# Forming sixteen MLP pieces inside the gelu pauses, and moving the normalising products from GpSimd to VectorE

## The chip, the cores and the metric

The kernel runs on one core of a Trainium2 chip. The metric is the device time of one execution in microseconds (us); lower is better. Five engines work side by side, each through its own instructions in order: TensorE (PE in the profile, PEld for its weight loads), VectorE (DVE), ScalarE (ACT), GpSimd (POOL) and SyncE (SP), which here only issues DMA transfers. Matmul results land in PSUM, eight banks of 128 partitions by 512 float32 values; GpSimd doesn't read PSUM here.

## The reference

An attention block and an MLP, both on the same layer-normalised input, and their sum.

```python
xn = _layernorm(x)                                   # x: 1 x 2048 x 512
# A: 32 heads of 16
qkv = (xn @ wqkv).reshape(B, S, 3, 32, 16).transpose(2, 0, 3, 1, 4)
p = softmax(einsum("bhqd,bhkd->bhqk", q, k) * 16 ** -0.5)
A = einsum("bhqk,bhkd->bhqd", p, v).transpose(0, 2, 1, 3).reshape(B, S, D) @ wo
# B: 512 -> 1792 -> 512
h = gelu(einsum("bsd,df->bsf", _layernorm(xn), w1) + b1, approximate=True)
return x + A + einsum("bsf,fd->bsd", h, w2) + b2
```

## The kernel before, in words

The attention is cut into 32 groups `g`: 4 query tiles `qt` of 512 queries, times 8 sets of 4 heads. A group has 16 key blocks of 128, and a unit is one head's 128 x 512 scores for one key block; there are 2048 units. A score pass (`qk`, line 1165; its matmul is line 1169) forms up to four units at once in different row strips of the array. A unit goes one of two ways.

- **ScalarE's way.** `build_tile` (1334) puts two or three units side by side in the scores' banks 0 to 4 and one ACTIVATE (line 1374) takes the exponentials.
- **VectorE's way.** `build_dve` (1459) takes a set of four units: each is shifted to integers from its bank (line 1471), then `dve_terms` makes three shifted copies of all four (line 1492, 2048 int16 columns), and the four versions are read as float16 and added up by four passes over the values. The scores of such a set ride along in a score pass of ScalarE's units, or go alone (`ride_alone`, 1299), and need a bank of the pool `misc` (banks 5 to 7).

Both end in `pv` (1179; matmul line 1187), which accumulates a group's output and its row sums in a `misc` bank. `build_opost` (1516) finishes a group: the bank is copied to `osb` (1527), the row sums go to DRAM and back as `lc`, VectorE takes reciprocals `rc` (1534), these go to DRAM and come back broadcast as `rlb`, and a product `osb * rlb` (1543) gives the normalised heads. That product is on GpSimd for the first 28 groups and on VectorE for the last three that pass here.

The MLP works on the same query tiles. `build_mlp` (1633) forms 14 pieces for each `qt`: `chain` (937) makes a piece's four matmul steps (sixteen matmuls, line 606) in a `misc` bank, and VectorE adds `b1` and writes it to `ht` (line 1655). The weights come through a ring of four buffers (`w1_r`, `NW1`). After every second query tile `fg` (1664) runs gelu in place over the 28 pieces of two tiles, as four ACTIVATEs of 3584 columns; exponentials stop for that time. `merge` (1688) multiplies by `w2` (and `wo`) and adds `acc`, which `sums` (1675) has filled by two GpSimd transfers for each 128 rows: `x`, and `b2` added in flight.

A planner (`_Plan`, `run` at 134) fixes the order of all instructions when the kernel is built: it simulates the engines with planned durations (0.60 us and more on VectorE, `GMUL = 2.1` for the product on GpSimd, `L1, L2, L3` for the transfers), and takes on each engine the ready operation of the least due time; the table `PICK` overrides single choices by their count on the engine. While TensorE would pause, `fill` (1783) issues matmuls over zeros (line 1813), and `zeros` (1322) adds one beside score passes (1329).

Of the kernel before, what the change touches and what calls it, by code (L numbers as in the profile page):

```python
# [11 lines left out]
ALU = mybir.AluOpType  # L12
# [48 lines left out]
class _Plan:  # L61
# [72 lines left out]
    def run(self):  # L134
        free = self.free = {e: 0.0 for e in self.ENGS}
        self.count = {e: 0 for e in self.ENGS}
# [6 lines left out]
        while self.left:  # L143
            best = None
            for e in self.ENGS:
# [7 lines left out]
                every = cand  # L153
# [3 lines left out]
                if e == "PE":  # L157
# [4 lines left out]
                    if hot:  # L162
# [5 lines left out]
                key = lambda c: (c[1].prio + self.nudge(c[1].seq)  # L168
                                 - (self.KEEP if c[1].mode == same else 0.0), c[1].seq)
                t, op = min((c for c in cand if c[0] <= first + tol), key=key)  # L170
                want = self.pick.get(e, {}).get(self.count[e])
                if want is not None:
                    t, op = next((c for c in every if c[1].seq == want), (t, op))
# [5 lines left out]
            self.count[op.eng] += 1  # L179
# [43 lines left out]
    nudge = staticmethod(lambda seq: 0.0)  # L223
# [264 lines left out]
def kernel(  # L488
# [133 lines left out]
    def act(cols):  # L622
# [10 lines left out]

    wide = {key: _Pool([res[i]]) for key, i in (
# [51 lines left out]
    TLAT, YP, YLAT = 2.6, 6.0, 4.2  # L686
    ZROW = 1
    DG = (3,)
    GMUL = 2.1
    YB = 17.0  # L690
# [17 lines left out]
    KT1, QT1 = 45.0, 55.0  # L708
    KTP, QTP = 55.0, 75.0
    HOT = 4  # L710
    XACT = 2
    F2 = 200.0
    CHUNK = 4
    HOLD = 75.0
# [1155 lines left out]
```

## Time and profile before

| | |
|---|---|
| median of 3 runs | 778.33 us (778.17 to 778.48) |
| profiled execution | 776.0 us, of which the span of instructions 774.2 us |
| busy, share of the span | PE 95%, ACT 96%, DVE 92%, POOL 14% |
| exponentials on ScalarE, line 1374 | 623 instructions, 702.2 us |
| VectorE's own sets, lines 1471 and 1492 | 520 and 390 instructions, 620.6 us |
| gelu on ScalarE, line 1669 | 8 instructions, 24.9 us, and two table loads of 1283 ns |
| products on GpSimd, line 1543 | 28 instructions, 39.2 us |

A row of instruction groups says line, engine, operation, written tile, read tiles and shapes, count, then the busy time, the mean duration of one in ns, and the idle time just before them. A matmul's end is modelled and matmuls overlap, so PE's 95% isn't its share of useful work. Neighbouring instructions of an in-order engine overlap a little too, so the distance between two starts is shorter than a duration.

### The profile page before, as it was taken

The numbers are of one execution on the slowest core, as the hardware profiler recorded it, in microseconds if no ns is written. First come the engines' busy times: TensorE is split into PE (matmuls) and PEld (weight loads), VectorE is DVE, ScalarE is ACT, GpSimd is POOL, SyncE is SP. The second block draws the span as 40 slices with busy tenths as digits, with TensorE's granted clock in tenths as the row PEclk, the third lists the DMA queues.
The fourth block names the chain that finished last, engine by engine and source line by source line (L and its number), as shares of the span: only waits on it lengthen the run. The fifth ranks groups of instructions, "written<-read, shape, count | busy, mean of one in ns | idle before, by whom it ended". The sixth has DMA issues, their size and how long they took to land.

```text
span 774.2 us, 23564 instructions
## 1 busy us (share of the span) xinstructions
PE 736.0 (95%) x10064; PEld 247.5 (32%) x10066; DVE 708.5 (92%) x1191; ACT 740.1 (96%) x651; POOL 105.5 (14%) x139
## 2 busy tenths in 40 slices
PE   8999999999999999999989999999999999999996
PEld 3434333333323323333322333323323223333332
DVE  8999999889999998998989998989999997899993
ACT  6999999999999999999998999999999999999995
POOL 5610101000021101000032000000213000110010
PEclk9999999999999999999999999999999999999998
DMA  6327111202323121100183211031332002122001
GB/s 218 71 70 171 56 46 42 64 18 60 90 50 74 55 56 36 39 25 30 39 163 78 49 31 39 18 93 50 88 90 59 18 19 56 53 72 53 17 16 34
DMA packets 77150, 46.56 MB, mean 60 GB/s; under 512 B 53429, under 2 KB 68213, under 8 KB 77041
## 3 DMA queue, kind: packets, MB, share of 16 engines
q1 hardware_dynamic: 70544, 33.48, 16.9%
q0 software_dynamic: 5536, 11.01, 5.6%
q8 instruction: 79, 1.29, 0.7%
q10 hardware_dynamic: 960, 0.52, 0.2%
q14 instruction: 31, 0.25, 0.1%
HBM read 30.01 MB, written 7.19 MB: 48 GB/s over the span
## 4 chain that ended last, share of the span: by engine, by line
PE 45%; DVE 24%; ACT 20%; issue 8%; DMA 2%; SPq 0%; POOL 0%; DVEq 0%; ACTq 0%
ACT p_sb L1374 20%; PE ps L1169 15%; PE ps L1187 15%; PE ps L606 13%; DVE x_sb L1471 10%; DVE it L1492 8%; DVE it L1471 1%; DMA lc<-ldram 1%; DMA ldram<-osb 1%; DVE ht L1655 1%; PE ps L1813 1%; DVE osb L1527 1%; PE ps L1742 0%; PE ps L611 0%; DVE ot L1693 0%
## 5 line engine op out<-in xcount | busy, mean ns | idle before, releaser
L1374 ACT ACTIVATE p_sb<-ps 128x1536 bf16<-128x1536 f32 (+1 forms) x623 | 702.2, 1257 | 18.7 <-PE ps L1169 16.0
L1169 PE MATMUL ps<-qz,kt 32*128 32x512 bf16 x2048 | 307.0, 383 | 20.0 <-ACT p_sb L1374 7.1
L1471 DVE TENSOR_SCALAR x_sb<-ps 128x512 int16<-128x512 f32 x412 | 274.1, 684 | 14.3 <-PE ps L1169 12.7
L1492 DVE TENSOR_SCALAR it<-x_sb 128x2048 int16<-128x2048 int16 x309 | 218.0, 722 | 4.1 <-PE ps L1187 2.3
L1169 PEld LDWEIGHTS <-kt 32*128 32x128 bf16 x2048 | 80.6, 91 | 257.7 <-issue 250.9
L1187 PE MATMUL ps<-p_sb,va 128*32 128x512 bf16 x1528 | 149.7, 389 | 2.0 <-DVE ht L1655 1.2
L1187 PE MATMUL ps<-it,va 128*32 128x512 f16 x1668 | 135.8, 381 | 2.1 <-DVE it L1492 2.0
L1187 PEld LDWEIGHTS <-va 128*32 128x32 bf16 x3608 | 78.0, 95 | 140.7 <-issue 114.8
L1329 PE MATMUL ps<-ones_bf,zeros_bf 32*128 32x512 bf16 x272 | 100.0, 383 | 0.0
L1471 DVE TENSOR_SCALAR it<-ps 128x512 int16<-128x512 f32 x108 | 72.9, 684 | 8.2 <-PE ps L1169 8.0
L606 PE MATMUL ps<-yT,w_r 128*32 128x512 bf16 x896 | 59.2, 384 | 2.8 <-DVE it L1471 1.6
L606 PE MATMUL ps<-w_sb,ht 128*32 128x512 bf16 x896 | 59.7, 381 | 0.0
L1492 DVE TENSOR_SCALAR it<-it 128x2048 int16<-128x2048 int16 x81 | 55.6, 702 | 0.6 <-PE ps L1187 0.3
L1543 POOL TENSOR_TENSOR ons<-osb,rlb 128x512 bf16<-128x512 f32 x14 | 19.4, 1383 | 238.1 <-DMA rlb<-rdram 145.6
L1543 POOL TENSOR_TENSOR ont<-osb,rlb 128x512 bf16<-128x512 f32 x14 | 19.8, 1418 | 217.3 <-DMA rlb<-rdram 196.4
L1655 DVE TENSOR_SCALAR ht<-ps,b_sb 128x512 bf16<-128x512 f32 x56 | 41.7, 745 | 1.1 <-PE ps L606 0.9
L1187 PE MATMUL ps<-x_sb,va 128*32 128x512 f16 x412 | 41.1, 385 | 1.5 <-DVE x_sb L1471 0.9
L1813 PE MATMUL ps<-ones_bf,zeros_bf 128*32 128x512 bf16 x468 | 39.7, 384 | 0.0
L606 PEld LDWEIGHTS <-w_r 128*32 128x32 bf16 x896 | 22.1, 96 | 26.3 <-issue 13.2
L1329 PEld LDWEIGHTS <-zeros_bf 32*128 32x128 bf16 x272 | 24.0, 91 | 19.3 <-issue 18.6
L606 PEld LDWEIGHTS <-ht 128*32 128x32 bf16 x896 | 20.2, 96 | 24.8 <-issue 11.5
L1669 ACT ACTIVATE ht<-ht 128x3584 bf16<-128x3584 bf16 x8 | 24.9, 3178 | 0.0
(101 smaller groups left out, 336.2 us busy)
## 6 DMA issues: line engine op xcount, KB each, us to landing
rlb<-rdram SPq DMA_DIRECT2D x31, 256.0 KB
w_r<-in_B_w_dram SPq DMA_DIRECT2D x56, 128.0 KB
wkv<-in_A_x_dram POOLq DMA_DIRECT2D x16, 256.0 KB, 3.6
wkv<-in_B_b_dram POOLq DMA_DIRECT2D x16, 256.0 KB, 4.2
qz<-zdram SPq DMA_DIRECT2D x30, 128.0 KB
ydram<-ys POOLq DMA_DIRECT2D x16, 128.0 KB, 2.1
zdram<-qc SPq DMA_DIRECT2D x15, 128.0 KB
w_sb<-in_B_w_dram SPq DMA_DIRECT2D x1, 1792.0 KB
```

Of the source, the lines that this page charges most:

```text
L606: I(nc.tensor.matmul(dst[32 * j:32 * j + 32], lhsT=lhsT[:, 32 * j:32 * j + 32], rhs=rhs, start=start, stop=stop, tile_position=(0, 32 * j)))
L1169: I(nc.tensor.matmul(ps[:, bank, :], lhsT=kt[lo:lo + 32, s // 2, k * P:(k + 1) * P], rhs=qz[lo:lo + 32, (qt * NB + s // 2) % NQB, s % 2, : ...
L1187: I(nc.tensor.matmul(ps[32 * j:32 * j + 32, o_bank[g], :], lhsT=vals[:, h * VS:h * VS + 32], rhs=wts(j), start=pv_done[g] == 1, stop=end, ...
L1329: I(nc.tensor.matmul(ps[:, o_bank[g], :], lhsT=zeros_bf[32 * j:32 * j + 32, :], rhs=ones_bf[32 * j:32 * j + 32, :], start=False, stop=Fals ...
L1374: exp_inst.append(I(nc.scalar.activation(p_sb[:, s0:s1, :].rearrange("p a b -> p (a b)"), ps[:, b0:b0 + n, :].rearrange("p a b -> p (a b)" ...
L1471: I(nc.vector.tensor_scalar(out=ib[sl][:, j, :], in0=ps[:, pool.bank(key), :], scalar1=LEVEL, scalar2=0.0, op0=ALU.add, op1=ALU.max))
L1492: I(nc.vector.tensor_scalar(out=tb[x].rearrange("p j q -> p (j q)"), in0=ib[sl].rearrange("p j q -> p (j q)"), scalar1=float(SHIFT[t]), sc ...
L1527: e0 = add("DVE", dve(QW), lambda: I(nc.vector.tensor_copy(osb[:, i2, :], ps[:, o_bank[g], :])), pvs + before, pr - 1000, rel=(o_done(g),))
L1543: lambda: I((nc.vector if late else nc.gpsimd).tensor_tensor(out=dst, in0=osb[:, i2, :], in1=rlb[:], op=ALU.mult)), [e3] + list(free),
L1655: I(nc.vector.tensor_scalar(out=hq[:, fc, :], in0=ps[:, misc.bank(key), :], scalar1=b1_sb[:, fc:fc + 1], scalar2=None, op0=ALU.add))
L1669: I(nc.scalar.activation(out=hv, in_=hv, func=AF.Gelu_apprx_tanh, scale=1.0))
L1813: I(nc.tensor.matmul(ps[32 * j:32 * j + 32, bank, :], lhsT=zeros_bf[:, 0:32], rhs=ones_bf[:], start=new, stop=new, tile_position=(0, 32 * ...
```

## The change

- **Pieces during gelu.** Of the 14 pieces of query tiles 1 and 3, the last eight (`ND`), sixteen in all, aren't formed before gelu any more. They are formed after the gelu instructions have begun, in the scores' banks 0 to 4 (pool `idle`), and ScalarE reads them there: one ACTIVATE of 512 columns each with `b1` as its bias. VectorE's addition for these pieces is gone. Gelu in place now covers the 14 pieces of the first tile (two ACTIVATEs of 3584 columns) and the six remaining of the second (two of 1536), set between the pieces.
- **Gates.** `q_gate` and `x_gate` hold score passes and exponentials back in the plan until these pieces are formed and read; `g_gate` and `d_gate` order gelu behind the last scored tile and the pieces behind gelu. `fill` may use the idle scores' banks.
- **Products.** `osb * rlb` is on VectorE for all groups (`GMUL` goes).
- **Sums.** One pair of transfers fills `acc` for all four row blocks of a query tile: 8 transfers where there were 32. The first of a pair waits for all four merges of the tile before.
- **Queues.** The sixteen writes of `ydram` and the two of zeros to `zdram` are issued by SP instead of GpSimd.
- **Order.** `PICK` is a new table, counted over all engines' steps together; `nudge` and `MIX` (all zeros) go. Due times of the MLP pieces move: `HA0..HB3`.

```diff
-                want = self.pick.get(e, {}).get(self.count[e])
...
+            want = self.pick.get(self.step)
+            self.step += 1
+            if want is not None:
+                op = next(o for r in ready.values() for o in r if o.seq == want)
+                t = max(self._start(op), free[op.eng])
...
+    idle = _Pool(res[:5])
...
+    ND, DS, DP = 8, 4, 2
-    GMUL = 2.1
...
-    HA0, HB0, HA1, HB1 = 0.36, 0.75, 0.65, 1.25
-    HA2, HB2, HA3, HB3 = 1.5, 1.9, 2.7, 3.1
+    HA0, HB0, HA1, HB1 = 0.46, 0.95, 0.95, 1.25
+    HA2, HB2, HA3, HB3 = 1.7, 2.4, 2.8, 3.1
...
-            yw_op[t] = add("POOL", 0.65, lambda t=t: I(nc.gpsimd.dma_start(
-                ydram[t * P:(t + 1) * P, :], ys[:, t % 2, :])), (y_op[t],), pr, lat=3.0)
+            yw_op[t] = dma("SP", ydram[t * P:(t + 1) * P, :], ys[:, t % 2, :], (y_op[t],), prio=pr,
+                           lat=2.5)
...
+    def q_gate(_, take=False, give=None):
+        g = phase["op"]
+        if g is not None and not take and (
+                phase["left"] if g.done else g.ndeps == 0 and g.ready <= I.now + GLEAD):
+            return None
+        return 0.0
...
-        late = g >= NG - LASTN
-        e4 = add("DVE" if late else "POOL", dve(QW) if late else GMUL,
+        e4 = add("DVE", dve(QW), lambda: I(nc.vector.tensor_tensor(
...
+            if qt % 2 and fc >= FC - ND:
+                last.append((fc, n, w))
+                continue
...
-            for i in range(2):
-                for h0 in (0, half):
-                    hv = ht[:, i, h0:h0 + half, :].rearrange("p a b -> p (a b)")
-                    I(nc.scalar.activation(out=hv, in_=hv, func=AF.Gelu_apprx_tanh, scale=1.0))
-        gelu[0] = add("ACT", act(2 * FC * QW) + 3.5, fg, h_ops + hs, hi + 4)
+            soft(0, 0, half)
+            soft(0, half, FC)
+        g = phase["op"] = add("ACT", act(FC * QW) + 1.5, fg, h_ops + hs, hi + 4, acq=((g_gate, None),))
+        for x, (fc, n, w) in enumerate(last):
...
+                for jc in range(JC):
+                    mm(ps[:, idle.bank(key), :], w1_r[:, n % NW1, jc, :], yT[:, jc, :], jc == 0, jc == JC - 1)
...
+                I(nc.scalar.activation(out=hq[:, fc, :], in_=ps[:, idle.bank(key), :],
+                                       func=AF.Gelu_apprx_tanh, bias=b1_sb[:, fc:fc + 1], scale=1.0))
...
+            f0, f1 = {DS: (0, rest // 2), DS + DP: (rest // 2, rest)}.get(x, (0, 0))
...
-    def sums(qi, pr):
+    def sums(qt, pr):
+        wait = [acc_op.get(c) for c in range(TQ)] + list(kt_op.values()) + list(va_op.values())
         xb_ = add("POOL", 1.0, lambda: I(nc.gpsimd.dma_start(
+            out=acc[:], in_=xv[:, qt * TQ:(qt + 1) * TQ, :])), wait, pr - 30, lat=XL + 3.0, nb=pr - 45)
+        return add("POOL", 1.2, lambda: I(nc.gpsimd.dma_start(
+            out=acc[:], in_=b2_all, accum_op=ALU.add)), (xb_,), pr - 20, lat=XL + 3.0)
```

## Rows read from the trace of the kernel before

**Rows 1.** The page's first part: busy us, share of the span, count.

```profile
PE 736.0 (95%) x10064; PEld 247.5 (32%) x10066; DVE 708.5 (92%) x1191; ACT 740.1 (96%) x651; POOL 105.5 (14%) x139
```

**Rows 2.** The chain that ended last, shares of the span by engine and by line.

```profile
PE 45%; DVE 24%; ACT 20%; issue 8%; DMA 2%; SPq 0%; POOL 0%; DVEq 0%; ACTq 0%
ACT p_sb L1374 20%; PE ps L1169 15%; PE ps L1187 15%; PE ps L606 13%; DVE x_sb L1471 10%; DVE it L1492 8%; DVE it L1471 1%; DMA lc<-ldram 1%; DMA ldram<-osb 1%; DVE ht L1655 1%; PE ps L1813 1%; DVE osb L1527 1%; PE ps L1742 0%; PE ps L611 0%; DVE ot L1693 0%
```

**Rows 3.** Waits: engine, line, releaser: total us, times, longest us.

```profile
ACT p_sb L1374 <- PE ps L1169: 16.0, 33, 2.4
...
DVE rc L1534 <- DMA lc<-ldram: 5.0, 5, 1.6
```

**Rows 4.** By stretch: length; PE, PEld, DVE, ACT, POOL busy us; clock; DMA; GB/s.

```profile
291.40:305.60 14.20, 13.36 (x155) 4.16 (x151) 14.12 (x24) 14.15 (x7) 1.69 (x2) 1.00 0.16 38
...
450.00:500.00 50.00, 49.38 (x681) 16.39 (x682) 44.10 (x74) 49.15 (x43) 2.55 (x2) 1.00 0.11 31
...
550.00:600.00 50.00, 48.30 (x589) 15.12 (x587) 49.81 (x83) 49.89 (x45) 13.70 (x15) 1.00 0.34 81
```

**Rows 5.** The same for line 606 alone (projections and MLP): PE, PEld.

```profile
450.00:500.00 50.00, 18.46 (x284) 6.67 (x288) 1.00 0.11 31
...
550.00:600.00 50.00, 8.36 (x128) 2.99 (x128) 1.00 0.34 81
...
sum 774.20, PE 184.70 PEld 76.02; mean PE 9.23 PEld 3.80
```

**Rows 6.** The same for line 1813 alone, the filling matmuls: PE, PEld.

```profile
291.50:307.00 15.50, 7.33 (x104) 2.29 (x104) 1.00 0.14 35
...
622.30:637.00 14.70, 4.92 (x64) 1.32 (x64) 1.00 0.07 21
```

**Rows 7.** PE in order of time, one MLP piece: start, us, instructions merged.

```profile
288.47 1.05 PE L606 MATMUL ps<-yT,w_r 128*32 128x512 bf16 x16
```

**Rows 8.** Groups of instructions, shapes kept apart.

```profile
L1655 DVE TENSOR_SCALAR ht<-ps,b_sb 128x512 bf16<-128x512 f32 x56 | 41.7, 745 | 1.1 <-PE ps L606 0.9
...
L1543 DVE TENSOR_TENSOR ont<-osb,rlb 128x512 bf16<-128x512 f32 x2 | 1.4, 682 | 0.0
...
L1492 DVE TENSOR_SCALAR it<-x_sb 128x2048 int16<-128x2048 int16 x309 | 218.0, 722 | 4.1 <-PE ps L1187 2.3
...
L1492 DVE TENSOR_SCALAR it<-it 128x2048 int16<-128x2048 int16 x81 | 55.6, 702 | 0.6 <-PE ps L1187 0.3
...
L1374 ACT ACTIVATE p_sb<-ps 128x512 bf16<-128x512 f32 x1 | 0.7, 678 | 0.0
...
L807 ACT ACTIVATE p_sb<-x_sb,nm 128x512 bf16<-128x512 bf16 x1 | 0.7, 721 | 0.0
...
L803 ACT ACTIVATE p_sb<-x_sb 128x512 bf16<-128x512 bf16 x1 | 0.6, 629 | 0.5 <-DMA x_sb<-in_A_x_dram 0.5
```

**Rows 9.** Line 1492 alone: duration ns min/median/max, first and last start.

```profile
L1492 DVE TENSOR_SCALAR it<-x_sb x309: 626/686/1773, 44.8 to 756.0; 128x2048 int16<-128x2048 int16 x155
```

**Rows 10.** A product on POOL, and DVE at the same time, in order of time.

```profile
82.23 1.27 POOL L1543 TENSOR_TENSOR ont<-osb,rlb 128x512 bf16<-128x512 f32 x1 [6.75 <-DMA rlb<-rdram]
...
82.28 1.77 DVE L1492 TENSOR_SCALAR it<-x_sb 128x2048 int16<-128x2048 int16 x1
```

**Rows 11.** DVE, then ACT in order of time: neighbours merged with their count.

```profile
297.06 1.29 DVE L1471 TENSOR_SCALAR x_sb<-ps 128x512 int16<-128x512 f32 x2
...
292.79 12.43 ACT L1669 ACTIVATE ht<-ht 128x3584 bf16<-128x3584 bf16 x4
```

**Rows 12.** Engines by stretch, columns as in the fourth group.

```profile
389.00:400.00 11.00, 10.00 (x111) 3.19 (x110) 10.96 (x18) 10.51 (x10) 5.22 (x7) 1.00 1.05 185
```

**Rows 13.** SP's issues, then ACT, in order of time around 400 us.

```profile
400.20 0.56 SPq L1529 DMA_DIRECT2D ldram<-osb  x1
404.36 0.35 SPq L1531 DMA_DIRECT2D lc<-ldram  x1
...
410.14 1.45 ACT L1374 ACTIVATE p_sb<-ps 128x1536 bf16<-128x1536 f32 x1 [2.43 <-PE ps L1169]
```

More of the change, by code (lines that the diff above doesn't have):

```diff
@@ L135, in run @@
         free = self.free = {e: 0.0 for e in self.ENGS}
-        self.count = {e: 0 for e in self.ENGS}
+        self.step = 0
         ready = self.ready = {e: [] for e in self.ENGS}
@@ L711 @@
     XACT = 2
+    GLEAD = 1.0
     F2 = 200.0
@@ L1021 @@
     mk_z0 = add("POOL", 0.9, lambda: I(nc.gpsimd.memset(ons[:], 0.0)), (), 0.0)
[L1022 to L1024 removed]
+    mk_z = [dma("SP", zdram[n].rearrange("(e p) q -> p e q", e=2), ons[:], (mk_z0,), prio=10.0, lat=3.0,
+                nb=16.0) for n in range(2)]
     def build_q(qt, b):
@@ L1332, in zeros, with x_gate, g_gate, d_gate @@
                 tile_position=(32 * j, 0), skip_group_check=True))
+    phase = {"op": None, "left": 0, "act": 0}
+    def q_gate(_, take=False, give=None):
[4 more added lines that the diff above has]
+        return 0.0
+    def x_gate(_, take=False, give=None):
+        g = phase["op"]
+        return None if g is not None and g.done and phase["act"] and not take else 0.0
+    def g_gate(_, take=False, give=None):
+        return 0.0 if scored[1].done else None
+    def d_gate(_, take=False, give=None):
+        return 0.0 if phase["op"].done else None
     def build_tile():
@@ L1361, in build_tile @@
             deps += qk_deps(g, k)
-        acq = [(res[b0 + x], ("t", i)) for x in range(n)] + [(ride(i, us), None)]
+        acq = [(q_gate, None)] + [(res[b0 + x], ("t", i)) for x in range(n)] + [(ride(i, us), None)]
         q = add("PE", pen(1), fqk, list(dict.fromkeys(deps)) + [qk_prev[0]], dl - QO, acq=acq, mode="q",
@@ L1377, in build_tile @@
         e = add("ACT", act(n * QW), fex, [q, exp_prev[0]] + list(dict.fromkeys(free)), dl,
-                rel=[res[b0 + x] for x in range(n)])
+                acq=((x_gate, None),), rel=[res[b0 + x] for x in range(n)])
         exp_prev[0] = e
@@ L1540, in build_opost @@
                  [e3, last_rlb[0]], pr - 500, lat=l3)
-        late = g >= NG - LASTN
-        e4 = add("DVE" if late else "POOL", dve(QW) if late else GMUL,
-                 lambda: I((nc.vector if late else nc.gpsimd).tensor_tensor(
-                     out=dst, in0=osb[:, i2, :], in1=rlb[:], op=ALU.mult)), [e3] + list(free),
-                 pr - (1000 if late else 0))
+        e4 = add("DVE", dve(QW), lambda: I(nc.vector.tensor_tensor(
+            out=dst, in0=osb[:, i2, :], in1=rlb[:], op=ALU.mult)), [e3] + list(free),
+            pr - (1000 if g >= NG - LASTN else 0))
         last_rlb[0] = e4
@@ L1640, in build_mlp @@
             nb=lo - 12)
-        hs, ms = [], []
+        hs, ms, last = [], [], []
         for fc in range(FC):
@@ L1672 @@
+        y_use[:] = ms
+        gelu[0] = g
     gelu = [None]
     ot_use, acc_op = {}, {}
-    def sums(qi, pr):
-        c = qi % TQ
-        wait = [acc_op.get(c)] + list(kt_op.values()) + list(va_op.values())
+    def sums(qt, pr):
+        wait = [acc_op.get(c) for c in range(TQ)] + list(kt_op.values()) + list(va_op.values())
         xb_ = add("POOL", 1.0, lambda: I(nc.gpsimd.dma_start(
-            out=acc[:, c, :], in_=x2[qi * P:(qi + 1) * P, :])), wait, pr - 30, lat=XL,
-            nb=pr - 45)
-        return add("POOL", 1.0, lambda: I(nc.gpsimd.dma_start(
-            out=acc[:, c, :], in_=b2_all, accum_op=ALU.add)), (xb_,), pr - 20, lat=XL)
+            out=acc[:], in_=xv[:, qt * TQ:(qt + 1) * TQ, :])), wait, pr - 30, lat=XL + 3.0, nb=pr - 45)
+        return add("POOL", 1.2, lambda: I(nc.gpsimd.dma_start(
+            out=acc[:], in_=b2_all, accum_op=ALU.add)), (xb_,), pr - 20, lat=XL + 3.0)
@@ L1698, in build_out @@
     def build_out(qt):
+        xb_ = sums(qt, at((O0, O1, O2)[qt]))
         for c in range(TQ):
@@ L1706, in build_out @@
             deps = [o for b in bs for o in on_op[qt * NS + 2 * b + 1]] + ld_wo + [
-                gelu[0], ld_w2, sums(qi, pr), ot_use.get(qi - 2)]
+                gelu[0], ld_w2, xb_, ot_use.get(qi - 2)]
             m = merge(("o", qi), c, qi, steps, deps, pr, ot[:, qi % 2, :], qt, bs)
@@ L1715, in build_down @@
         del h_use[qt % 2][:]
+        xb_ = sums(qt, qts(qt, DN0))
         for c in range(TQ):
@@ L1719, in build_down @@
             steps = [(ht[:, qt % 2, fc, cs], w2_sb[:, fc, :]) for fc in range(FC)]
-            h_use[qt % 2].append(merge(("m", qi), c, qi, steps, [gelu[0], ld_w2, None, sums(qi, pr)], pr,
+            h_use[qt % 2].append(merge(("m", qi), c, qi, steps, [gelu[0], ld_w2, None, xb_], pr,
                                        acc[:, c, :], qt, ()))
@@ L1799, in fill @@
                     spot = [r.index for r in misc.res if r.holder is None and r.free_at <= t]
+                    if not spot and phase["act"]:
+                        spot = [r.index for r in idle.res if r.holder is None and r.free_at <= t]
                     if not spot and not scored[1].done and t + 0.516 < max(t1, gelu_end[0] - 1.2):
@@ L1810, in fn @@
                 bank = spot[0] if spot else o_bank[opened]
-                new = bool(spot) and bank >= 5
+                new = bool(spot) and not (bank < 5 and spot[0] is scored[0] and not scored[1].done)
                 for j in range(HS):
```

47 lines of the change are left out of this document (26 added, 21 removed), and 67 rows, old and new, of the table PICK.

## The prediction

> **What bounds the kernel now.** I read the busy shares first: TensorE, VectorE and ScalarE are all above 90% [rows 1], so no engine alone is the bound, and an average over the span can't say what a shorter step is worth. The chain that ended last says more. It runs 45% over TensorE, 24% over VectorE and 20% over ScalarE [rows 2]: work goes round in a loop, scores on TensorE, exponentials on ScalarE or shifts on VectorE, then the sums on TensorE. ScalarE waits only 16.0 us in all, and for score passes [rows 3]. So the time is mostly the exponentials that ScalarE has to take, and how many these are depends on how many sets VectorE takes off it.
>
> Two stretches show what holds VectorE back. Between 450 and 500 us it is busy 44.10 us while line 606 (projections and MLP) takes 18.46 us of TensorE; between 550 and 600 us it is busy 49.81 while line 606 takes 8.36 [rows 4, 5]. A piece in the making takes TensorE's time and a `misc` bank, and both are what VectorE's score units need. In the gelu stretch it is different: VectorE is full, 14.12 of 14.20 us [rows 4], and TensorE fills with matmuls over zeros, 7.33 and 4.92 us around the two gelus [rows 6]. There it has time to give.
>
> My sums weigh a step on an engine by the part of that kind of work that lies on the chain. Line 606: 13% of 774.2 us is 100.6 of its 184.7 us [rows 2, 5], a weight of 0.54. VectorE as a whole: 24% is 185.8 of 708.5 us [rows 1, 2], a weight of 0.26. Line 1655: 1% is 7.7 of 41.7 us [rows 2, 8], 0.19. This is a choice: the chain is one path through a loop that is nearly tight everywhere, so the ends, weight 0 and weight 1, go into the range.
>
> **The change part by part.**
>
> *Sixteen pieces leave the busy stretches.* One piece is 1.05 us on TensorE [rows 7], sixteen are 16.8 us. They go where 12.3 us of filling stood [rows 6]. Cover: if TensorE had no room there, they would lengthen gelu. At weight 0.54 that is -9.1 us; ends 0 (ScalarE is the bound) and -16.8.
>
> *Their additions on VectorE go.* 16 x 0.745 = 11.9 us [rows 8], at 0.19: -2.2; ends 0 and -11.9.
>
> *Gelu in pieces.* Four ACTIVATEs of 3584 columns take 12.43 us one behind the other [rows 11], 0.444 us for each 512 columns. A piece read from PSUM alone takes more: the one exponential of 512 columns is 678 ns, and an ACTIVATE with a bias from memory takes 721 ns where one without takes 629, so 92 more: 770 ns [rows 8]. Neighbours overlap, as the gelus do, so I take the middle, 0.61. Eight pieces then cost 8 x (0.61 - 0.444) = 1.3 us more for each gelu, 2.7 us in all; ends 0 and 16 x 0.326 = +5.2. This is paid in full, since exponentials stand still meanwhile. The table loads stay two for each gelu; the load back to exponentials stands between the last piece and the first exponential, and its time covers the score pass that waits for the last banks. Were that cover gone, each gelu would lose one score pass and its wait, in size like the 16.0 us over 33 waits [rows 3], 0.5 us.
>
> *Do the pieces come in time?* The weight ring has four buffers, so the last four weight loads are issued only when the first four pieces are formed, 4.2 us [rows 7] into gelu. ScalarE comes to the fifth piece after two long ACTIVATEs, four pieces and one of 1536 columns, about 6.2 + 2.4 + 1.3 = 9.9 us. A load has 5.7 us, and I price this at nothing.
>
> *Products on VectorE.* 28 more at 0.682 us, the three that are there already [rows 8]: 19.1 us; at 0.26 +5.0; ends 0 and +19.1.
>
> *No products on GpSimd beside VectorE's copies.* A copy on line 1492 that starts 0.05 us after a GpSimd product lasts 1.77 us [rows 10], where the median is 686 ns and the longest 1773 [rows 9]. The means are 722 and 702 ns [rows 8]; means less median, 309 x 0.036 + 81 x 0.016, give 12.4 us of lengthening that the planner doesn't know of. At 0.26 that is -3.3; ends 0 and -12.4.
>
> *More waits on VectorE.* The products now wait there for `rlb`, and behind a late one stands everything of VectorE: shifts, copies, additions, and then TensorE, which wants their banks and values. The trace of before has no such wait on VectorE except for the reciprocals: 5.0 us over 31 of them, five late [rows 3], and the three products without any [rows 8]. Like the reciprocals, 28 x 0.16 = 4.5 us, at 0.26 +1.2. Upper end: one late reciprocal near 400 us held VectorE 1.6 us at most [rows 3], and ScalarE then stood 2.43 us [rows 13], so 4.5 x 1.5 = +6.8; lower end 0.
>
> *Sums and queues.* Fewer and larger transfers cost no engine time on the path; GpSimd is busy 105.5 us [rows 1] and issues them with nothing behind that hurries. The first of each pair waits for four merges instead of one, tens of us ahead of the next tile's due time. Writes of `ydram` and zeros go past SP's queue near the start, eighteen issues of about half a microsecond as SP's others [rows 13]; their cover is that SP mostly waits for VectorE. I take 0, between one stall less and two more of 2.43 us [rows 13].
>
> *Order.* A new table can't be priced from the trace. ScalarE's waits for scores, 16.0 us [rows 3], are all that an order alone could give back; I take 0 and give it a few us either way.
>
> **Sum.** -9.1 - 2.2 + 2.7 + 5.0 - 3.3 + 1.2 = -5.7 us. The profiled execution took 776.0 us, 774.2 of it the span; it would take 770.3. The median of the runs is 778.33, 2.3 above it, and I take the difference to that: 772.6 us.
>
> **A rule on the queues.** While the sums' transfers, a transposing transfer and weight loads keep the DMA engines full between 389 and 400 us [rows 12], an 8 KB transfer issued at 400.20 lets its successor go only at 404.36 [rows 13]. The Trainium skill, "DMA: Bandwidth & Descriptors", section "Queues, rings and completion order", says that each DMA engine goes round its queues packet by packet. By that rule a larger transfer on GpSimd's queue would not make SP's small ones later than a smaller one does, and the time would be the sum, 772.6; what the row shows, a small transfer that was 4 us late beside large ones, is the ground of the slower rival. I don't trust the rule far enough to drop it.
>
> **The rivals.**
>
> *VectorE uses all that it is given* (chance 0.15). For 10.1 us more of line 606 VectorE was busy 5.7 us less [rows 4, 5]. With 16.8 us taken out it would win 9.5 us, two sets more of about 4.7 us (four shifts at 0.65 [rows 11], three copies at 0.70 [rows 9]). Two sets are eight units, 8 x 0.46 = 3.7 us of exponentials (702.2 us for the 1528 units that the 520 on VectorE leave). If the lengthening also counts in full, -12.4 in place of -3.3, the end is 759.8; half of both gives 766.2. For it: VectorE is the in-order neighbour of all others. Against: a planned order rarely gets all.
>
> *ScalarE is the bound* (0.13). It is busy 96% [rows 1]. Then VectorE's terms don't count, TensorE's relief counts by what ScalarE waits: 16.0 x 16.8 / 184.7 = 1.5 us, and gelu costs 2.7: 779.5. Against it: ScalarE's share of the chain, 20%.
>
> *Late transfers stop VectorE* (0.17). The sums come as 1 MB of `acc` twice for each query tile, eight bursts, and VectorE now waits for two transfers in each group, `lc` and `rlb`. Where a burst meets one, VectorE stands and ScalarE loses 2.43 us [rows 13]. Three such meetings use up the gain, 772.6 + 7.3 = 779.9; five give 784.8. For it: the row at 400 us is such a meeting. Against: the reciprocals met it rarely, five of 31 [rows 3].
>
> *The pieces come late* (0.03). If weights or banks aren't there in time, ScalarE waits inside gelu: 3 us each time give 778.6.
>
> **How the numbers follow.** The forecast has 0.52. About 0.2%, 1.6 us, is what a measurement of this kernel can tell from no change. Faster by more: forecast and first rival, 0.67. Within it: ScalarE the bound and late pieces, 0.16. Slower: late transfers, 0.17. The range of 764 to 781.5 us holds the forecast with its terms' ends, most of the first rival, the two within the bound and the mildest meetings; it leaves out the far part of the first and most of the late transfers, some 0.17 together.
>
> **What would show it.** In the changed kernel's trace: sixteen ACTIVATEs of 512 columns with gelu, steps near 0.6 us, and a gelu stretch of about 14 us between its table loads; line 1655's successor 40 times instead of 56; hardly any filling matmuls during gelu; line 1492's mean within 10 ns of its median; 31 products on VectorE, with waits for `rlb` of a few us in all; VectorE's sets at 130 or a few more. I am wrong if the gelu stretch is 3 us longer than that, if VectorE's waits for `lc` and `rlb` exceed 10 us, or if ScalarE's waits for scores don't fall although line 606 has moved.

## The result and the profile after

The changed kernel takes 786.59 us (783.75 to 787.99) where the kernel before took 778.25 on the same chip: a ratio of 1.0104, 95% interval 1.008 to 1.0127, 1.0% slower. 772.6 was forecast, with a range that ended at 781.5. The forecast had the wrong sign. Medians below are of all executions of a kernel; ratios and their intervals leave out those more than 1.5% longer than the kernel's shortest.

The page of the changed kernel, its first part and its chain by engine, to be laid beside [rows 1, 2]:

```profile
PE 737.8 (94%) x10011; PEld 247.5 (32%) x10013; DVE 711.2 (91%) x1217; ACT 736.9 (94%) x663; POOL 38.3 (5%) x69
...
PE 34%; ACT 33%; DVE 16%; issue 11%; DMA 5%; SPq 0%; DVEq 0%; ACTq 0%
```

Busy time hardly differs between the kernels, apart from GpSimd's products. The chain does: ScalarE's share has gone from 20% to 33% and TensorE's from 45% to 34%, DMA from 2% to 5% and "issue" from 8% to 11%. The waits, as in [rows 3] (engine, line, releaser: total us, times, longest us), show who stands:

```profile
ACT p_sb L1380 <- PE ps L1160: 29.1, 34, 9.2
...
DVE rc L1540 <- DMA lc<-ldram: 12.1, 2, 8.6
...
PE ps L604 <- DVE x_sb L1477: 8.5, 2, 8.3
...
DVE ont L1547 <- DMA rlb<-rdram: 0.5, 1, 0.5
```

ScalarE waits for score passes 29.1 us instead of 16.0, nearly as often (34 times to 33), so a few waits have become long. VectorE waits 12.1 us in only two reciprocals. Beside them the parts of the change can be read from the groups, as in [rows 8]:

```profile
L1380 ACT ACTIVATE p_sb<-ps 128x1536 bf16<-128x1536 f32 (+1 forms) x619 | 696.5, 1263 | 30.9 <-PE ps L1160 29.1
...
L1498 DVE TENSOR_SCALAR it<-x_sb 128x2048 int16<-128x2048 int16 x315 | 212.6, 693 | 4.2 <-PE ps L1178 3.2
...
L1664 DVE TENSOR_SCALAR ht<-ps,b_sb 128x512 bf16<-128x512 f32 x40 | 30.0, 750 | 2.7 <-PE ps L604 2.7
L1851 PE MATMUL ps<-ones_bf,zeros_bf 128*32 128x512 bf16 x368 | 32.3, 382 | 0.0
```

The bias additions are 40 instead of 56. The copies, now line 1498, last 693 ns in the mean instead of 722. The exponentials, now line 1380, are four fewer than the 623 of before (702.2 us of them, as the first rival has it), and 5.7 us shorter together. One gelu stretch, ScalarE in order of time, to be laid beside [rows 11]:

```profile
270.41 1.28 ACT L1676 ACT_TABLE_LOAD   x1
271.70 6.27 ACT L1676 ACTIVATE ht<-ht 128x3584 bf16<-128x3584 bf16 x2
277.88 2.40 ACT L1694 ACTIVATE ht<-ps,b_sb 128x512 bf16<-128x512 f32 x4
...
285.36 1.28 ACT L1380 ACT_TABLE_LOAD   x1
286.65 1.02 ACT L1380 ACTIVATE p_sb<-ps 128x1024 bf16<-128x1024 f32 x1
```

From the first table load to the next exponential it takes 16.24 us. Before, the load stood at 291.50 and the next exponential at 306.54, 15.04 us. So gelu costs 1.2 us more each time, with no wait inside.

The profiled execution took 784.31 us, 8.3 more than the 776.0 of before. Waits for scores +13.1, two gelus +2.4 and exponentials -5.7 make +9.8, all on ScalarE, and that is the whole difference within 1.5 us. So the question is where the 13.1 us of waits come from. The longest, 9.2 us, is found by following the chain in order of time near 400 us (start, us, what):

```profile
394.64 9.89 DMA ldram<-osb
...
404.59 3.03 DMA lc<-ldram
...
407.64 0.25 DVE rc L1540
407.90 0.56 DVE x_sb L1477
...
408.50 1.90 PE ps L604 x12
```

and GpSimd's issues just ahead of it, in order of time (`acc` uses the memory of `wkv`, so transfers into `acc` bear that name):

```profile
386.27 0.77 POOL L1714 DMA_DIRECT2D wkv<-in_A_x_dram  x1 [165.69 <-DVE ot L1727]
392.20 1.28 POOL L1716 DMA_DIRECT2D wkv<-in_B_b_dram  x1 [5.17 <-DMA wkv<-in_A_x_dram]
```

An 8 KB transfer takes 9.89 us, its successor 3.03. The reciprocal stands in front of VectorE's queue, the shift behind it frees a bank for TensorE, and ScalarE gets no scores. The pair of merged sum transfers was issued just before, as soon as the last `acc` block was free. VectorE stands again at 525 us, beside the next pair. The chain there, then GpSimd's issues:

```profile
515.71 4.36 DMA ldram<-osb
...
520.09 5.04 DMA lc<-ldram
...
518.95 1.22 POOL L1714 DMA_DIRECT2D wkv<-in_A_x_dram  x1 [108.13 <-DVE ot L1727]
525.59 1.53 POOL L1716 DMA_DIRECT2D wkv<-in_B_b_dram  x1 [5.42 <-DMA wkv<-in_A_x_dram]
```

Here only x, the first of the pair, was on its way beside `lc`: it was issued when `ldram` was nearly through, and the accumulating one only at 525.59, after `lc` had landed. What the stalls do to TensorE stands in the table by stretch, columns as in [rows 4]:

```profile
400.00:408.00 8.00, 0.21 (x3) 0.09 (x1) 0.36 (x2) 1.86 (x2) 0.14 (x1) 0.73 0.52 120
408.00:412.00 4.00, 3.50 (x31) 0.90 (x30) 3.23 (x6) 0.96 (x1) 2.66 (x4) 0.50 0.09 19
...
416.00:420.00 4.00, 3.93 (x56) 1.54 (x56) 3.91 (x8) 3.72 (x5) 0.00 (x0) 1.00 0.17 37
...
528.00:536.00 8.00, 7.73 (x63) 1.54 (x59) 5.81 (x10) 4.95 (x4) 0.00 (x0) 0.50 1.20 163
```

TensorE was busy 0.21 of 8.00 us, and then its granted clock is 0.50, the lower of its two levels (1.2 of 2.4 GHz), until past 412. A piece that took 1.05 us [rows 7] took 1.90. In the second stall it ran at the lower level all through 528 to 536, and ScalarE's waits there show it, in order of time:

```profile
526.71 1.02 ACT L1380 ACTIVATE p_sb<-ps 128x1024 bf16<-128x1024 f32 x1 [2.13 <-PE ps L1160]
529.40 2.56 ACT L1380 ACTIVATE p_sb<-ps 128x1536 bf16<-128x1536 f32 x2 [1.67 <-PE ps L1160]
532.88 1.45 ACT L1380 ACTIVATE p_sb<-ps 128x1536 bf16<-128x1536 f32 x1 [0.92 <-PE ps L1160]
534.82 1.02 ACT L1380 ACTIVATE p_sb<-ps 128x1024 bf16<-128x1024 f32 x1 [0.49 <-PE ps L1160]
537.12 3.71 ACT L1380 ACTIVATE p_sb<-ps 128x1536 bf16<-128x1536 f32 x3 [1.27 <-PE ps L1160]
```

The theory after this reading: the merged sum transfers cost the whole loss and more, by making small transfers late and by what TensorE's clock adds. The rival: the loss is in the other parts (gelu, products on VectorE, the order), and the sums' transfers only happen to lie there.

### The profile page after: what moved, and what is told of

Its sections match the earlier page's. It is cut to its first block, busy times and chain, and to the rows that moved or that the text cites. A ratio compares the mean times of both kernels' runs of the same rounds, so it can differ in the third digit from the quotient of the medians.

```text
span 782.5 us, 23385 instructions
## 1 busy us (share of the span) xinstructions
PE 737.8 (94%) x10011; PEld 247.5 (32%) x10013; DVE 711.2 (91%) x1217; ACT 736.9 (94%) x663; POOL 38.3 (5%) x69
## 4 chain that ended last, share of the span: by engine, by line
PE 34%; ACT 33%; DVE 16%; issue 11%; DMA 5%; SPq 0%; DVEq 0%; ACTq 0%
ACT p_sb L1380 29%; PE ps L1178 11%; PE ps L1160 11%; PE ps L604 10%; DVE x_sb L1477 6%; DVE it L1498 5%; ACT ht L1676 2%; DMA ldram<-osb 2%; DMA w_r<-in_B_w_dram 1%; DVE it L1477 1%; ACT ht L1694 1%; DMA lc<-ldram 1%; DVE ht L1664 1%; PE ps L1851 1%; DVE osb L1533 1%
## 5 line engine op out<-in xcount | busy, mean ns | idle before, releaser
L1380 ACT ACTIVATE p_sb<-ps 128x1536 bf16<-128x1536 f32 (+1 forms) x619 | 696.5, 1263 | 30.9 <-PE ps L1160 29.1
L1160 PE MATMUL ps<-qz,kt 32*128 32x512 bf16 x2048 | 310.8, 385 | 23.3 <-ACT p_sb L1380 11.5
L1477 DVE TENSOR_SCALAR x_sb<-ps 128x512 int16<-128x512 f32 x420 | 280.0, 687 | 20.7 <-PE ps L1160 19.9
L1498 DVE TENSOR_SCALAR it<-x_sb 128x2048 int16<-128x2048 int16 x315 | 212.6, 693 | 4.2 <-PE ps L1178 3.2
L1315 PE MATMUL ps<-ones_bf,zeros_bf 32*128 32x512 bf16 x294 | 108.3, 386 | 0.0
L604 PEld LDWEIGHTS <-w_r 128*32 128x32 bf16 x896 | 21.0, 97 | 37.8 <-issue 20.3
L1664 DVE TENSOR_SCALAR ht<-ps,b_sb 128x512 bf16<-128x512 f32 x40 | 30.0, 750 | 2.7 <-PE ps L604 2.7
L1851 PE MATMUL ps<-ones_bf,zeros_bf 128*32 128x512 bf16 x368 | 32.3, 382 | 0.0
L1315 PEld LDWEIGHTS <-zeros_bf 32*128 32x128 bf16 x294 | 25.8, 91 | 14.4 <-issue 13.3
L1533 DVE COPY osb<-ps 128x512 f32<-128x512 f32 x31 | 21.3, 688 | 2.1 <-PE ps L1178 2.1
L1714 POOL DMA_DIRECT2D wkv<-in_A_x_dram x4 | 3.8, 962 | 388.5 <-DVE ot L1727 388.5
L1540 DVE RECIPROCAL rc<-lc 128x16 f32<-128x16 f32 x31 | 7.7, 248 | 12.1 <-DMA lc<-ldram 12.1
```

The source lines that it names most:

```text
L604: I(nc.tensor.matmul(dst[32 * j:32 * j + 32], lhsT=lhsT[:, 32 * j:32 * j + 32], rhs=rhs, start=start, stop=stop, tile_position=(0, 32 * j)))
L1160: I(nc.tensor.matmul(ps[:, bank, :], lhsT=kt[lo:lo + 32, s // 2, k * P:(k + 1) * P], rhs=qz[lo:lo + 32, (qt * NB + s // 2) % NQB, s % 2, : ...
L1315: I(nc.tensor.matmul(ps[:, o_bank[g], :], lhsT=zeros_bf[32 * j:32 * j + 32, :], rhs=ones_bf[32 * j:32 * j + 32, :], start=False, stop=Fals ...
L1380: exp_inst.append(I(nc.scalar.activation(p_sb[:, s0:s1, :].rearrange("p a b -> p (a b)"), ps[:, b0:b0 + n, :].rearrange("p a b -> p (a b)" ...
L1477: I(nc.vector.tensor_scalar(out=ib[sl][:, j, :], in0=ps[:, pool.bank(key), :], scalar1=LEVEL, scalar2=0.0, op0=ALU.add, op1=ALU.max))
L1498: I(nc.vector.tensor_scalar(out=tb[x].rearrange("p j q -> p (j q)"), in0=ib[sl].rearrange("p j q -> p (j q)"), scalar1=float(SHIFT[t]), sc ...
```

## The experiments

In the diffs a minus stands before lines of the kernel that a run starts from (the changed one or the one before) and a plus before those of the run.

**The sums' transfers away.** *a4_no_sums* is the changed kernel, order kept:

```diff
-        xb_ = add("POOL", 1.0, lambda: I(nc.gpsimd.dma_start(
-            out=acc[:], in_=xv[:, qt * TQ:(qt + 1) * TQ, :])), wait, pr - 30, lat=XL + 3.0, nb=pr - 45)
-        return add("POOL", 1.2, lambda: I(nc.gpsimd.dma_start(
-            out=acc[:], in_=b2_all, accum_op=ALU.add)), (xb_,), pr - 20, lat=XL + 3.0)
+        xb_ = add("POOL", 1.0, lambda: I(nc.gpsimd.memset(acc[:], 0.0)) if qt == 0 else None,
+                  wait, pr - 30, lat=XL + 3.0, nb=pr - 45)
+        return add("POOL", 1.2, lambda: None, (xb_,), pr - 20, lat=XL + 3.0)
```

> The changed kernel with its order kept, but without any of the eight sums' transfers: acc is set to zero once, so x and b2 are left out of the output. Theory 'late transfers': in the changed kernel ScalarE stands 10.5 us around 411 to 415 us and 6.5 us between 526 and 537, each behind a reciprocal that waits on VectorE for lc while the sums' transfers of 1 MB run. Without them about 17 us go, against 786.6: 769 to 771 us, and the reciprocals' waits fall from 12.1 us to under 1. Theory 'parts': the pieces, the products or the new order are themselves dearer than forecast: 783 to 787 us, the standing times go elsewhere.

It took 766.34 us, a ratio of 0.9843 (0.9821 to 0.9866) to before. The waits of its profile:

```profile
ACT p_sb L1380 <- PE ps L1160: 12.0, 30, 2.5
...
DVE rc L1540 <- DMA lc<-ldram: 0.3, 1, 0.3
```

At the second stall's place `lc` takes 1.64 us here instead of 5.04, while `ldram`, 4.39 us, is as slow without any sums. ScalarE's waits fall by 17.1 us, and the run's profiled execution is 17.9 us shorter than the changed kernel's. The transfers cost 20 us of the median, and the rival falls. But the kernel before has sums too. *b5_no_sums* takes them out there in the same way:

> The kernel before with its order kept and without the 32 sums' transfers: acc is set to zero, x and b2 are left out of the output. With the changed kernel without sums (766.3) it gives what the pieces, the products and the order are worth without the transfers. If the forecast's terms hold (5.7 us): 771 to 773 us, before having lost some 4 to 6 us to its one stall. If the other parts are worth nothing: 766 us. If they are worth more than forecast: 775 to 778.

It took 773.70 us, 0.9953 (0.9935 to 0.997). The sums cost the kernel before 3.6 us and the changed kernel 20. Without sums the rest of the change is worth 0.9843 / 0.9953 = 0.989, 8.5 us of gain, where the forecast had 5.7.

**What about the transfers harms.** The next runs keep all bytes but order or place them differently, or leave one half out. *a2_split*: the changed kernel, with four transfers of 256 KB for x and then four for b2 where one of 1024 KB each stood.

```diff
+            for c in range(TQ):
+                I(nc.gpsimd.dma_start(out=acc[:, c, :], in_=xv[:, qt * TQ + c, :]))
...
+            for c in range(TQ):
+                I(nc.gpsimd.dma_start(out=acc[:, c, :], in_=b2_one, accum_op=ALU.add))
```

> The changed kernel with its order kept; each pair of 1 MB sums' transfers issued at the same place as four pairs of 256 KB. If the size of one transfer is what holds the small ones back: both stalls shrink to the 2.4 us that the kernel before showed once, 773 to 777 us. If the amount in flight at that time is what counts: 784 to 788 us, no change, since the same bytes go at the same time. By the rule on packets in the Trainium skill, 'DMA: Bandwidth & Descriptors', section 'Queues, rings and completion order', the size of a transfer doesn't matter, so the second.

780.53 us, 1.0015 (0.9997 to 1.0032): between the two. ScalarE still stands 6.67 us at 404; there the transfer into `ldram` was issued only at 399.80, behind SP's weight loads, and took 4.71 us. *a6_pairs*: each block's b2 transfer directly behind its x transfer, so that the next block's pair is issued only as that block comes free:

```diff
+def fpair():
+    for c in range(TQ):
+        I(nc.gpsimd.dma_start(out=acc[:, c, :], in_=xv[:, qt * TQ + c, :]))
+        I(nc.gpsimd.dma_start(out=acc[:, c, :], in_=b2_one, accum_op=ALU.add))
```

> The changed kernel with its order kept, but each row block of 128 has its own pair of 256 KB sums' transfers (x, then b2) directly behind each other on GpSimd's queue, so that each pair starts as soon as its own block of acc is free, some 20 us apart, and not all at the last merge. Theory 'too much at one time': no transfer meets more than 512 KB of sums, the time comes near that without sums, 767 to 771 us. If any sums' transfer beside a small one does the harm, however small: eight and more shorter stalls, 776 to 781 us, as with all x first and all b2 behind (780.5).

771.54 us, 0.9913 (0.9882 to 0.9943). Same bytes, same queue, 15 us less. Only the first tile's four pairs, whose blocks are all free from the start, still come at once, and there one stall is left, behind a late weight load (`w_r`), TensorE and then ScalarE in order of time:

```profile
239.22 1.90 PE L604 MATMUL ps<-yT,w_r 128*32 128x512 bf16 x16 [3.54 <-DMA w_r<-in_B_w_dram]
...
241.77 2.36 ACT L1380 ACTIVATE p_sb<-ps 128x1536 bf16<-128x1536 f32 x2 [4.58 <-PE ps L1160]
```

*a7_spaced* holds the later pairs of that tile back on exponentials as well:

```diff
+if qt == 0 and c:
+    later.append((I.now + 16.0 * c, lambda c=c: pair(c)))
+else:
+    pair(c)
```

> The changed kernel with each 128-row block's two sum transfers directly behind each other (as in the run that gave 771.54 us), and in the first query tile the pairs of blocks 1 to 3 held back on exponentials, some 16 us apart, where that run issued all four together at 212 to 236 us and ScalarE then waited 4.58 us at 242 for a late weight load (4.13 us for w_r). If sum transfers that queue up behind each other are what makes small loads late, that wait goes and the time is 766 to 769. If the load was late for another reason, it stays, and the time is 770 to 772.

766.59 us, 0.987 (0.9845 to 0.9895): the stall is gone, and with all its sums the kernel is by the medians as fast as it was without any (766.34); by the ratios to before, 0.987 and 0.9843, it is some 2 us slower, with intervals that overlap. It beats both kernels. Its waits:

```profile
ACT p_sb L1380 <- PE ps L1160: 12.4, 28, 2.4
...
DVE rc L1544 <- DMA lc<-ldram: 2.4, 2, 1.8
```

*a1_no_b2* leaves out the accumulating halves alone:

```diff
-        return add("POOL", 1.2, lambda: I(nc.gpsimd.dma_start(
-            out=acc[:], in_=b2_all, accum_op=ALU.add)), (xb_,), pr - 20, lat=XL + 3.0)
+        return add("POOL", 1.2, lambda: None, (xb_,), pr - 20, lat=XL + 3.0)
```

> The changed kernel with its order kept and without the four accumulating transfers of the second bias (b2 is left out of the result); the four 1024 KB transfers of x stay. Without both the time was 766.34, with both 786.59. If the accumulating half does the harm (11.2 us from issue to landing against 6.4 us for x), the time is 768 to 772. If the transfer of x does, it is 779 to 785. If both harm by their bytes, 775 to 778.

771.6 us, 0.9922 (0.9887 to 0.9956). By the medians a megabyte of x alone costs some 5 us against none, the second megabyte behind it 15. But the seven executions split: three took 765.28 to 767.35 us at a mean granted clock of 0.998 to 1.000, four took 771.6 to 773.91 at 0.991 to 0.993. The profiled one is the shortest, and in such an execution x alone costs nothing; what lowers the clock in the others no trace shows. Does the second megabyte harm because it accumulates? *a8_plain_b2* sends the same bytes without accumulating:

```diff
-            out=acc[:], in_=b2_all, accum_op=ALU.add)), (xb_,), pr - 20, lat=XL + 3.0)
+            out=acc[:], in_=b2_all)), (xb_,), pr - 20, lat=XL + 3.0)
```

> The changed kernel with the four transfers of the second bias writing plainly in place of accumulating (x is left out of the result): the same 1024 KB from the same place behind the same transfer. Without them the time was 771.6, with them 786.59. If accumulating is what harms, the landing time falls from 11.2 us towards the 6.4 us of x, and the time is 770 to 775. If one more megabyte harms by its bytes, the time stays at 782 to 787.

782.01 us, 1.0062 (1.0042 to 1.0082). By the medians 4.6 of the 15 us hang on the accumulating, the other 10.4 on the bytes; by the ratios it is 3.3 of 14.2, and the intervals of this run and of the changed kernel just overlap. So the bytes are the larger part, and a share of the accumulating is hardly clear of noise. The issues of both kernels, the changed one first (KB each, median us to landing), and the chain of a8_plain_b2 in order of time:

```profile
wkv<-in_B_b_dram POOLq DMA_DIRECT2D x4, 1024.0 KB, 11.2
```

```profile
wkv<-in_B_b_dram POOLq DMA_DIRECT2D x4, 1024.0 KB, 10.1
...
398.27 6.63 DMA ldram<-osb
```

The landing time stays near 10 us, far from the 6.4 of x, and the small transfer still takes 6.63 (the profiled execution is the longest of its seven, 789.04 us). The same transfer took 3.96 us in a7_spaced and 2.37 in a1_no_b2. In the latter x had landed before it was issued (384.52 + 5.6 against 392.77), so 2.37 is its time beside none of the sums, close to the 2.66 of a4_no_sums. *a9_later* keeps the merged accumulating pairs and issues those of the second and third tile 30 us later:

```diff
+later.append((I.now + (0.0, 30.0, 30.0, 0.0)[qt], whole_pair))
```

> The changed kernel with its merged pairs of the second and third query tile issued 30 us later (held on an exponential), away from the transposing load and the first quarter's reciprocals. If the harm is the meeting with those transfers, the stalls of ScalarE of 9.18 us at 411 and of 6.5 us in all at 525 to 536 go, and the time is 769 to 775. If a merged pair harms wherever it lies (each cycle of small transfers takes some 10 of every 20 us, so it meets another one), the stalls move with it and the time stays at 782 to 788.

771.3 us, 0.9926 (0.9905 to 0.9946). The stalls at 411 and 525 are gone, and a smaller one takes their place, the chain and then ScalarE:

```profile
433.69 5.78 DMA ldram<-osb
...
448.57 7.01 ACT L1380 ACTIVATE p_sb<-ps 128x1536 bf16<-128x1536 f32 x6 [3.63 <-PE ps L1160]
```

At this place in the order, with no sums (a4_no_sums), SP issued the transfer at 434.27 and its successor at 436.00, so it took 1.73 us at most. So most of the harm is the place: two megabytes right beside a tile's transposing load (issued at 387.76 in the changed kernel) and the reciprocals' transfers behind it. What is left against a7_spaced, 4.7 us by the medians, is what merging still costs in this better place.

**Merging alone, in the order of before.** *b1_merged_sums*:

```diff
-            out=acc[:, c, :], in_=x2[qi * P:(qi + 1) * P, :])), wait, pr - 30, lat=XL,
+            out=acc[:], in_=xv[:, qt * TQ:(qt + 1) * TQ, :])), wait, pr - 30, lat=XL + 3.0,
...
-            out=acc[:, c, :], in_=b2_all, accum_op=ALU.add)), (xb_,), pr - 20, lat=XL)
+            out=acc[:], in_=b2_all, accum_op=ALU.add)), (xb_,), pr - 20, lat=XL + 3.0)
```

> The kernel before with the changed kernel's one large pair of sum transfers for a query tile (1024 KB each, issued when all four blocks are free) in place of four pairs of 256 KB, and nothing else of the change. If merging the pairs is what harms, here too ScalarE waits behind late small transfers, and the time rises by 5 to 12 us to 782 to 790. If it harms only together with the new order (which puts the transposing load and the first reciprocals' transfers next to it), the time stays within 2 us of 778.

783.27 us, 1.0091 (1.0064 to 1.0119): slower, as the first case had it, but not by its mechanism. The profiled execution, the shortest of six, took 779.77 us, 3.8 more than before's. No wait of ScalarE there is over 2.1 us, and the reciprocals wait 3.7 us in all. The plan came out differently around the longer transfer: near 400 us the second transfer was issued 18 us after the first (408.00 and 390.08), and VectorE's shifts into `x_sb` are 408 where they were 412, one set less. ScalarE's exponentials are 2.6 us longer together (704.8) and its waits 1.0 us (17.0), nearly the whole 3.8. That run doesn't price merging by itself.

**The largest term.** *c1_twice16* is the kernel before with sixteen MLP pieces' matmuls issued twice (the second issue starts the sum anew):

```diff
+if twice:
+    for y, (a, b) in enumerate(part):
+        mm(ps[:, pool.bank(key), :], a, b, f0 + y == 0, f0 + y == len(steps) - 1)
```

> The kernel before with sixteen MLP pieces' matmuls issued twice (32 matmuls of 128x512 instead of 16 in each; these pieces' results are not the reference's): 16 x 1.05 = 16.8 us more work for TensorE and nothing else changed. It prices the forecast's largest term, TensorE relieved of sixteen pieces between exponentials at a weight of 0.54, without leaving TensorE idle. By that weight the time rises by 9.1 us to some 787. If ScalarE alone set the pace there, it stays at 778 to 779. If TensorE did without gaps, it rises by the full 16.8 to 794 or 795.

785.29 us, against 776.27 for before in the same runs: 9.0 us for 16.8 us of added work, a weight of 0.54. The opposite, *b2_no16*, leaves the sixteen pieces' matmuls out:

```diff
+                if empty:
+                    return misc.bank(key)
```

> The kernel before with its order kept, without the matmuls of the sixteen pieces (the last eight of query tiles 1 and 3; their additions read what the bank holds, so the MLP's output is wrong). It prices 16.8 us of TensorE's work in the busy stretches by itself. By the weight from the chain, 0.54: 769 us. If ScalarE is the bound: 776 to 777 us. At full weight: 761 us.

785.45 us, 1.0039 (1.0009 to 1.007): less work, and slightly slower. The executions scatter with the clock, from 776.34 us at a mean granted clock of 0.992 to 789.82 at 0.970 and one of 854.23 at 0.748. By stretch of the profiled one, 600 to 680 us, without the pieces and then in the kernel before:

```profile
600.00:680.00 80.00, 73.61 (x816) 20.78 (x817) 66.86 (x109) 72.65 (x57) 7.13 (x7) 0.89 0.13 36
```

```profile
600.00:680.00 80.00, 76.72 (x980) 24.04 (x976) 72.17 (x117) 77.80 (x61) 8.83 (x8) 1.00 0.13 36
```

TensorE has less to do, its granted clock falls to 0.89 in the mean, ScalarE gets 57 ACTIVATEs through instead of 61. The run can't price the relief: its time holds the relief and the fall of the clock together.

**The products.** *b3_dve_products* is the kernel before with all products on VectorE:

```diff
-lambda: I((nc.vector if late else nc.gpsimd).tensor_tensor(
+I(nc.vector.tensor_tensor(out=dst, in0=osb[:, i2, :], in1=rlb[:], op=ALU.mult))
```

> The kernel before with 28 products on VectorE at the place in the order where GpSimd had them; the rest of the order is kept, so VectorE has 19.1 us that the plan doesn't know of, and no lengthened copies. If these weigh alike, one in-order engine's time against the other: 12.4 less, 19.1 more, weight as VectorE's share: 780 us. If lengthened copies are worse than planned work, being unknown in place: 770 to 776. If a wait for rlb on VectorE at an unplanned place stalls all: 784 and more.

774.02 us, 0.9959 (0.9945 to 0.9974): 3.2 us faster, though VectorE has 19 us more to do that the plan doesn't know of. Copies and products there:

```profile
L1492 DVE TENSOR_SCALAR it<-x_sb 128x2048 int16<-128x2048 int16 x309 | 206.3, 683 | 3.9 <-PE ps L1187 2.4
...
L1544 DVE TENSOR_TENSOR ont<-osb,rlb 128x512 bf16<-128x512 f32 x16 | 10.9, 682 | 0.5 <-DMA rlb<-rdram 0.5
```

The copies' mean falls from 722 ns [rows 8] to 683, and the longest from 1773 ns [rows 9] to 823. *a3_pool_products* moves 28 products of the changed kernel back to GpSimd:

```diff
-        e4 = add("DVE", dve(QW), lambda: I(nc.vector.tensor_tensor(
+            late = g >= NG - LASTN
...
+            I((nc.vector if late else nc.gpsimd).tensor_tensor(
```

> The changed kernel with its order kept, but 28 products on GpSimd again, at the place in the order where VectorE had them. By the forecast's terms VectorE wins 5.0 us and loses 3.3 to lengthened copies: 784 to 786 us. If waits for rlb on VectorE were a cause of the loss: 780 or less, with VectorE's and ScalarE's standing around 411 and 526 us shorter. If the lengthened copies count in full: 792 to 799 us.

794.25 us, 1.0199 (1.0174 to 1.0224): 7.7 us slower than the changed kernel, with three waits for `lc`, 16.4 us in all, where there were two, 12.1. To keep the sums out of it, *a5_no_sums_pool* does the same without them:

> The changed kernel without sums' transfers (x and b2 left out) and with 28 products on GpSimd again, order kept: prices the products' part without the stalls, against 766.3. By the forecast (5.0 more, 3.3 less): 764 to 766. By the run with sums, where GpSimd's products cost 7.7 us more: 773 to 775, the lengthened copies counting nearly in full.

The median was 780.24 us, 1.0004 (0.9969 to 1.0039), but the executions lie between 770.5 at a mean granted clock of 0.999 and 783 at 0.982. At equal clock that is some 4 us above a4_no_sums; the longer executions are those of a lower clock. The profiled one, the longest of the twelve, shows one such fall, VectorE in order of time and then the engines by stretch:

```profile
218.73 3.43 DVE L1498 TENSOR_SCALAR it<-x_sb 128x2048 int16<-128x2048 int16 x1
...
224.00:252.00 28.00, 28.00 (x193) 5.16 (x193) 17.56 (x29) 18.28 (x16) 0.00 (x0) 0.52 0.30 51
```

One copy beside a product of GpSimd (218.60 to 219.87) and behind it the clearing of `acc`, 1.80 us, which this run has in place of the sums, took 3.43 us instead of 0.68. TensorE stood 2.63 us behind it, and then ran 28 us at the lower level, and ScalarE was busy 18.28 of them.

## Why the prediction was wrong, point by point

- *Sums and queues* is the step that failed. It took 0, between -2.4 and +4.9, with the reason that the first transfer of a pair waits for four merges "tens of us ahead of the next tile's due time". The due time was never in danger; what the pair met was another's transfer. Measured, the sums cost 20.3 us in the changed kernel and 3.6 in the one before, so the term is +16.7.
- *The rival that named the mechanism*, late transfers that stop VectorE, was right in kind and too cheap. It priced a meeting at 2.43 us, the one stall that before had [rows 13]. The two here cost ScalarE 9.18 + 0.48 + 0.81 = 10.5 and 2.13 + 1.67 + 0.92 + 0.49 + 1.27 = 6.5 us. The row of before was a meeting with three accumulating transfers of 256 KB each, issued between 395.99 and 398.98, and from it the price of one with 1024 KB was taken unscaled. Nor did it have the clock: the lower level that follows an idle TensorE. Its count, three to five, was too high, and 784.8 came near 786.59 by two errors that cancel.
- *The rule on the queues.* The sentence from the Trainium skill, "DMA: Bandwidth & Descriptors", section "Queues, rings and completion order", on engines that go round their queues packet by packet, was taken to mean that a larger transfer on GpSimd's queue would not make SP's small ones later. The traces don't agree with that reading: 2.37 us with none of the sums on its way, 9.89 with the second megabyte (a1_no_b2 and the changed kernel). Whether in the first stall the small transfer itself waited for packets of the pair, or for its own queue's transposing load that the pair slowed, no run tells apart. A transposing load isn't needed for a delay: in a9_later it was issued at 386.49, 47 us ahead, and the small transfer beside the pair took 5.78 us, where it took 1.73 at most without sums. In the second stall, too, it was issued only at 527.51, after `lc` had taken 5.04 us beside x. In a1_no_b2, with x issued 0.8 us ahead of it as well, the same transfer took 2.07, so what made it that late stays open.
- *Sixteen pieces*, -9.1 at weight 0.54: c1_twice16 measured 9.0 us for 16.8 of added work. For added work the weight read from the chain held; the relief itself no run priced. The pieces did take the place of filling matmuls, 368 instead of 468.
- *Additions, gelu.* 40 additions as said; their weight wasn't measured. Gelu cost 2.4 us, 2.7 forecast; four pieces took 2.40 us, 0.60 each (0.61 forecast). They never came late.
- *Products, lengthened copies, waits* were +5.0, -3.3 and +1.2, together +2.9. Measured -3.2 in the order of before and -7.7 in the new one. The second figure is from a run with the sums' stalls; without sums it is some 4 us at equal clock. The wrong part is the one weight, 0.26, for both. In b3_dve_products VectorE got 19.1 us of products and lost 13.3 of lengthening (309 x 0.039 + 81 x 0.016), 5.8 us more work, and the time fell, so a microsecond of lengthening costs more than one in a product. Why isn't shown. That the planner knows of a product and not of a lengthened copy can't be the reason there, since that run's order was planned with the products on GpSimd. What it fits is that single long copies went (1773 ns at most before, 823 there): one of 3.43 us, beside a product and the clearing of `acc`, stood ahead of the fall of the clock in a5_no_sums_pool. The waits for `rlb` were 0.5 us, not 4.5.
- *VectorE uses all that it is given* happened as that rival said: 528 score units on VectorE instead of 520, two sets, and exponentials shorter by 5.7 us (3.7 forecast).
- *Order* wasn't run by itself. Pieces -9.0, gelu +2.4 and products -3.2 make -9.8; without sums the whole rest measured -8.5. These figures come from different kernels and leave out the additions and the two sets, so what the order is worth, apart from where it puts the sums' transfers, stays open.

The signs named for being wrong came true: waits for `lc` and `rlb` of 12.6 us, above the 10 named, and ScalarE's waits did not fall.

## What to carry to other kernels

A background transfer is not free because nothing waits for it: look at which small transfers with a waiter lie within its landing time, and price a meeting by the transfer's size and by what the stall does to TensorE's clock. Issue such traffic in small pieces, apart in time, each as its buffer comes free; the same bytes cost 20 us merged and 0 to 2 us spaced. The Trainium skill, "DMA: Bandwidth & Descriptors", section "Rules for kernel authors", advises to coalesce many small transfers into one large transfer, and names 64 KB as the size below which one pays mostly overhead. For blocks of 256 KB in a kernel that waits for small transfers on another queue these runs show the reverse: 786.59 us merged, 780.53 in pieces at the same place, 766.59 in pieces apart in time.

## What the runs showed of the hardware

- An 8 KB transfer on SP's queue took 2.37 us when the megabyte of x on GpSimd's queue had landed (a1_no_b2), 9.89 us with a second, accumulating one on its way (the changed kernel) and 6.63 with a plain one (a8_plain_b2), a transposing load and three weight loads standing ahead of it on SP's queue each time. With two weight loads ahead and no transposing load near it took 5.78 us beside an accumulating megabyte (a9_later), 1.73 at most beside none (a4_no_sums).
- After 8 us with TensorE busy 0.21 us its granted clock stood at the lower level until past 412 us, and after a shorter gap at 525 it stayed there from 528 to 536 although TensorE was busy 7.73 of the 8 us. With work taken from TensorE it was 0.89 in the mean over 80 us where it had been 1.00, and the kernel was no faster (b2_no16).
- One VectorE copy of 0.68 us lasted 3.43 us beside two operations of GpSimd (1.27 and 1.80 us, one execution of a5_no_sums_pool), another 1.77 us beside one product of 1.27 [rows 10]. With no product on GpSimd the longest took 823 ns (b3_dve_products) and 1033 (the changed kernel).
